# A gated linear recurrence and a spectral filter on one core: another DFT, other bonus path, other load path, other order

## The chip, the cores and the metric

The kernel runs on one core of a Trainium2 chip. A core has a matrix engine (PE, TensorE), a vector engine (DVE), a scalar engine (ACT), GpSimd (POOL), and SyncE (SP), whose queue issues the transfers here. Each engine runs its own queue in order; semaphores order the engines against one another. Matmul results land in PSUM; SBUF holds everything else. The metric is the time of one execution in microseconds.

## The reference, cut to what matters

```python
B, H, S, D = 4, 8, 768, 48
for t in range(S):                                   # per batch and head
    cur = einsum('bhd,bhe->bhde', u[None] * k[t], v[t])
    y[t] = einsum('bhd,bhde->bhe', r[t], state + cur)
    state = w[t][..., None] * state + einsum('bhd,bhe->bhde', k[t], v[t])
x = y as (B, S, 384)
x1, x2, x3 = split(x @ w_proj, 3)                    # three times 384 columns
conv = irfft(rfft(x2) * rfft(filter_fft))            # circular, over S = 768
out = (x1 * conv * x3) @ w_out
```

The term `u * k * v` of the present step is called the bonus: for a token and a head it is v times the number sum(r * u * k).

## The kernel before, in words

**Chunks.** The 768 tokens of a batch are six chunks of 128, so there are 24 chunks (0 to 23; chunk c belongs to batch c // 6). For each chunk SP loads w, k, r and v as [128 tokens, 8, 48] in fp32 (`ldw`, `ldk`, `ldr`, `ldv`, L384), into rings of five buffers. ACT takes the logarithm of w (`lw`); PE forms the running sums with triangular masks (`cs`, `ce`); ACT exponentiates (`en`, `eq`, `ph`, the last being the decay over the chunk); DVE or POOL multiply (`kh`, `q`); PE transposes both (`tqk`), a copy brings them to SBUF (`tT`), PE forms the scores (`sc`), DVE masks them (`mt`). The state goes from chunk to chunk by `kv` (PE) and `S` (DVE). The bonus is `rk` (r times k), `rku` (times u, L439), `cc` (a sum over 48 columns on DVE, L442), `vc` (times v, L448). `y` adds on PE the bonus (an identity matmul, L499), the state's part (L502) and the scores' part (L507). `xn` copies y, `yt` transposes it, `xT` stores it; for the second half of a batch `sa` and `sb` form the sum and the difference of the two halves of the sequence.

**The spectral part**, per batch, after its six chunks: `p1`, `p3` (products with w_proj, L539) and `x1`, `g` (their copies and their product); `x2` (L562) and `ab` for the sum and difference halves; `f` (L348, L356), the forward DFT as six row blocks ("slots") of 128 frequencies, real and imaginary ones in turn; `X` copies it. The filter's spectrum comes the same way, once: `ldfilt`, `fs`, `fd`, `hf`, `H`, `hg`. The product of two spectra is four products and two sums (`ua` to `ud`, L584; `pr`, L589; `pi`, L593), each 1152 columns wide for batches 0 to 2 and 384 for batch 3. The inverse DFT is `iE` and `iO` (L602), four matmuls each for each of three column blocks; `ec` copies, `s` and `d` (L617, L622) form the sum and difference, `yy` (L627) multiplies by the gate, `po` (L634) by w_out, `o` copies, `st` stores (L643). The basis of the inverse is made from that of the forward transform by transposes (`m2t`, L324).

**Order.** Nothing is ordered by loops: `ORDER` (L36) is a list of some 1070 words such as `P:po.1.3@3`, that is engine, operation, its indices, and for PE the PSUM bank. Each engine issues its words in the order in which they stand. Six banks are handed out by number, and two together hold the scores (`@8`). Waits follow from data, and from buffers that are used again. Eight matmuls on zeros run ahead of everything (L687). w_proj and w_out are loaded by POOL's queue, which converts them to bf16 on the way (L312, L317).

Of the kernel before, what the change touches and what calls it, by code (L numbers as in the profile page):

```python
# [20 lines left out]
L = 128  # L21
# [5 lines left out]
HALF = S // 2  # L27
NT = HALF // L
UNIT = 65536.0
NEG = -29952.0  # L30
WARM = 8

# [4 lines left out]
A:tLn0 S:ldu G:masks S:ldw1 S:ldk0 S:ldw0 G:iota S:ldw2 S:ldk2 V:ang2 S:ldk1 V:ang0 S:ldw3  # L37
V:ang1 S:ldv1 A:lw2 A:lw0 P:cs2@0 P:ce2@1 S:ldr1 P:ce0@2 A:eq2 A:lw1 S:ldr0 P:ce1@3 P:cs1@4
P:cs0@5 A:eq1 S:ldr2 A:eq0 A:en1 S:ldv0 A:en0 V:kh1 A:ph2 A:lw3 G:kh0 A:en2 S:ldk3 A:v1 V:kh2
A:ph0 A:sin S:ldw5 V:q0 V:rk0 P:tqk0@4 S:ldw6 V:q1 G:q2 V:tT0 S:ldv2 V:rku0 G:v0 P:tqk2@5 V:cc0  # L40
P:cs3@1 S:ldr3 V:rk2 P:kv0@0 G:vc0 P:sc0@8 V:S0 P:ce3@2 V:mt0 S:ldw4 G:rku2 A:tT2 G:rk1 S:ldv3
V:cc2 P:y0@4 A:lw5 P:sc2@8 A:eq3 V:xn0 P:tqk1@0 A:en3 S:ldk4 V:rku1 G:v2 A:ph1 P:yt0@5 P:cs5@4
V:cc1 P:kv1@1 A:xT0 V:mt2 S:ldk6 A:lw6 G:rk3 A:ph3 A:tT1 S:ldr4 V:S1 G:vc2 A:lw4 V:vc1 P:kv2@3
A:en5 G:q3 S:ldv4 P:sc1@8 V:kh3 P:cs6@5 P:cs4@2 P:ce6@0 A:en4 G:rku3 P:y2@1 S:ldw8 V:S2 P:ce5@4
V:xn2 A:eq5 S:ldr5 G:v3 A:eq6 V:mt1 P:yt2@2 G:kh4 P:ce4@3 A:ph6 P:tqk3@1 S:ldr6 A:eq4 V:cc3
G:rk4 A:xT2 P:y1@4 V:tT3 S:ldk5 A:xn1 V:q4 G:rku4 P:sc3@8 P:m2t3@0 S:ldw7 P:m2t0@2 V:mt3
P:tqk4@1 P:yt1@4 A:tT4 S:ldr8 V:m2c3a G:q5 V:cc4 A:en6 V:vc3 P:m2t5@1 S:ldv7 P:sc4@8 A:xT1 G:rk6
A:lw8 P:y3@5 A:ph4 A:m2c3b S:ldr7 V:kh5 P:ce8@4 A:xn3 P:cs8@3 V:v4 V:mt4 P:tqk5@0 G:vc4 S:ldv5
P:yt3@5 A:tT5 G:rk5 V:sa3 S:ldk8 V:sb3 A:lw7 P:kv3@0 A:eq8 S:ldv6 V:S3 G:kh6 A:xT3 A:m2c5
P:ce7@0 P:sc5@8 G:q6 S:ldw11 A:eq7 P:y4@5 V:mt5 P:kv4@1 G:rku5 A:xn4 S:ldw9 A:en8 P:m2t2@5  # L50
V:rku6 G:v5 A:m2c0 V:S4 P:yt4@3 S:ldk7 G:q7 P:tqk6@2 V:cc6 V:sa4 A:tT6 V:cc5 S:ldk9 G:kh8 V:sb4
V:vc5 A:v7 G:q8 S:ldv8 A:ph8 A:v6 V:xT4 A:lw11 V:rk8 P:kv6@1 A:m2c2a P:sc6@8 S:ldw10 G:ldwp
P:m2t4@2 P:cs7@4 P:y5@3 A:en7 S:ldr9 A:lw9 V:xn5 G:kh7 V:S6 P:yt5@4 P:cs9@3 G:rk7 P:tqk8@1 V:sa5
V:mt6 A:tT8 G:vc6 V:sb5 A:m2c2b G:v8 V:rku8 P:tqk7@1 A:xT5 G:rku7 P:ce9@5 A:en9 P:y6@4 A:m2c4
P:sc8@8 A:xn6 V:cc7 A:ph7 A:eq9 V:cc8 P:yt6@3 P:cs11@2 A:lw10 P:kv7@4 V:mt8 G:vc8 A:tT7 P:ce10@0
S:ldv9 V:vc7 A:xT6 P:sc7@8 V:S7 P:cs10@1 S:ldw12 P:ce11@3 V:kh9 A:en10 P:y8@4 V:mt7 A:ph9 A:en11
S:ldr10 A:eq11 P:p1.0.2.1@1 V:xn8 P:y7@5 V:x1.0.2.1 S:ldk10 G:rk9 P:p1.0.1.0@2 A:xn7 P:yt8@3
S:ldv10 A:xT8 P:yt7@4 V:v9 P:kv8@1 V:rku9 A:xT7 P:p1.0.0.1@5 V:S8 P:x2.0.1.1@3 S:ldr11 A:lw12
V:x1.0.1.0 P:kv9@4 A:x1.0.0.1 V:q9 P:x2.0.0.2@1 A:eq10 S:ldk11 V:ab.0.1.1 P:m2t1@2 P:x2.0.0.1@5
V:ab.0.0.2 P:p1.0.0.0@3 S:ldw14 G:rk10 P:p1.0.2.0@1 A:x1.0.0.0 V:x1.0.2.0 P:tqk9@3 S:ldv13 G:q10  # L60
# [48 lines left out]
V:sa21 P:p3.2.2.0@1 V:xT22 V:sb21 P:p1.3.2.0@2 V:ub.2.0 A:xT21 P:y23@0 V:g.2.2.0 P:po.0.2@4
V:X.2.4 A:x1.3.2.0 P:po.0.5@1 A:xn23 V:ua.2.0 G:uc.2.0 P:x2.3.1.1@5 P:iE.1.0@2 V:o.0.5 V:o.0.2  # L110
# [25 lines left out]
def kernel(  # L136
# [104 lines left out]
    def nth(c):  # L241
        return (c - c // NCH) % 3
# [477 lines left out]
```

## Time and profile before

| what | value |
|---|---|
| median of 3 runs | 187.91 us (187.36 to 188.9) |
| span of the profiled execution | 186.7 us; no other time is given for that execution |
| busy: PE, DVE, ACT, POOL | 154.7, 159.5, 117.3, 107.4 us |
| instructions | 4118 |
| moved by DMA | 26.41 MB |

A row of a group of instructions reads: line, engine, operation, output and inputs with their shapes, count, then busy time in us and the mean of one in ns, then the idle time of the engine just before them and what ended it. A window's row gives for a stretch of time the busy time of each engine with its number of instructions, then the granted clock of PE, the share of the time in which the 16 DMA engines were busy, and the traffic. A row of SP's queue gives start, duration, and the transfer issued.

### The profile page before, as it was taken

What the parts mean: (1) busy time and instruction counts of PE and PEld (TensorE: products, weight loads), DVE (VectorE), ACT (ScalarE), POOL (GpSimd) and SP (SyncE); (2) the same over time, 40 slices, a digit from 0 to 9 for tenths busy, and PEclk for the clock granted to TensorE, in tenths of its full rate; (3) what the DMA queues carried; (4) which work ended last, traced back from release to release, by engine and by line L of the source; (5) the groups of instructions that cost most, each with busy time, mean ns of one, the idle gap of its engine ahead of it and who ended that gap; (6) DMA issues with size and microseconds to landing.
All of it is one profiled execution on the core that took longest, in us unless ns stands there. A gap on an engine that the chain in (4) does not pass through costs nothing.

```text
span 186.7 us, 4118 instructions
## 1 busy us (share of the span) xinstructions
PE 154.7 (83%) x1526; PEld 97.8 (52%) x1526; DVE 159.5 (85%) x302; ACT 117.3 (63%) x257; POOL 107.4 (57%) x120
## 2 busy tenths in 40 slices
PE   5147787665799988897977799999999999999971
PEld 2115456444666546563655555756556655556630
DVE  6829989786989799989998979999998999699760
ACT  2289756976585497697486969988356415531532
POOL 6024899398651482995995636636651866781000
PEclk9999999995589999999999969999999999999999
DMA  4999999999999983999999890400001000335336
GB/s 104 202 219 201 192 188 205 199 177 197 193 195 188 213 172 76 196 191 214 176 248 241 172 203 5 63 4 0 0 4 42 0 0 4 126 125 214 130 144 235
DMA packets 105043, 26.41 MB, mean 141 GB/s; under 512 B 100288, under 2 KB 104640, under 8 KB 105024
## 3 DMA queue, kind: packets, MB, share of 16 engines
q1 hardware_dynamic: 104224, 24.98, 61.0%
q0 software_dynamic: 800, 1.18, 3.8%
q8 instruction: 12, 0.20, 0.4%
q14 instruction: 7, 0.06, 0.1%
HBM read 22.61 MB, written 4.72 MB: 146 GB/s over the span
## 4 chain that ended last, share of the span: by engine, by line
PE 56%; DVE 24%; ACT 9%; issue 4%; DMA 3%; SPq 2%; ACTq 0%
PE p L539 10%; PE po L634 6%; DVE mt L474 5%; PE iE L602 4%; PE iO L602 4%; PE f L356 4%; PE x L562 4%; ACT qkT L229 3%; PE tqk L454 3%; PE sc L467 3%; DVE cc L442 3%; PE y L507 2%; DVE S L492 2%; PE f L348 2%; DVE rku L439 2%
## 5 line engine op out<-in xcount | busy, mean ns | idle before, releaser
L539 PE MATMUL p<-xT,wproj 128*128 128x384 bf16 x144 | 30.0, 330 | 2.3 <-DVE S L492 2.0
L474 DVE TENSOR_TENSOR mt<-sc,mask_excl 128x1024 bf16<-128x1024 f32 x24 | 29.1, 1214 | 2.2 <-PE sc L467 2.2
L448 POOL TENSOR_TENSOR vc<-v,cc 128x384 bf16<-128x384 bf16 x19 | 16.8, 887 | 18.0 <-DVE cc L442 6.3
L430 POOL TENSOR_TENSOR qk<-ldk,en 128x384 bf16<-128x384 f32 x15 | 16.0, 1068 | 17.3 <-ACT phi L424 9.0
L436 POOL TENSOR_TENSOR rk<-ldr,ldk 128x384 bf16<-128x384 f32 x18 | 20.1, 1118 | 6.7 <-DVE rku L439 5.6
L229 ACT ACTIVATE qkT<-tqk 128x1024 bf16<-128x1024 bf16 x19 | 19.5, 1029 | 6.2 <-PE tqk L454 6.0
L454 PE MATMUL tqk<-ident,qk 128*128 128x128 bf16 x192 | 16.8, 238 | 5.0 <-POOL qk L430 2.1
L539 PEld LDWEIGHTS <-wproj 128*128 128x128 bf16 x144 | 13.0, 98 | 11.5 <-issue 4.4
L433 POOL TENSOR_TENSOR qk<-ldr,eq 128x384 bf16<-128x384 f32 x13 | 14.1, 1085 | 7.2 <-ACT eq L418 4.8
L229 ACT ACTIVATE x<-p 128x384 bf16<-128x384 f32 x20 | 9.6, 492 | 12.9 <-PE p L539 10.2
L454 PEld LDWEIGHTS <-qk 128*128 128x128 bf16 x192 | 13.2, 106 | 8.1 <-issue 4.0
L390 ACT ACTIVATE lg<-ldw 128x384 bf16<-128x384 f32 x24 | 12.7, 532 | 6.0 <-DMA ldw<-in_w_dram 5.9
L634 PE MATMUL po<-wout,y 128*128 128x384 bf16 x72 | 14.3, 326 | 1.3 <-DVE y L627 1.1
L412 ACT ACTIVATE en<-cs 128x384 f32<-128x384 f32 x24 | 11.7, 496 | 5.3 <-PE cs L394 5.2
L562 PE MATMUL x<-wproj,sd 128*128 128x384 bf16 x72 | 14.8, 326 | 0.0
L555 DVE TENSOR_TENSOR g<-p,x 128x384 bf16<-128x384 f32 x24 | 13.0, 549 | 1.8 <-PE p L539 1.8
L394 PE MATMUL cs<-lg,mask_incl 128*128 128x384 bf16 x24 | 9.5, 413 | 5.3 <-ACT lg L390 4.6
L418 ACT ACTIVATE eq<-ce 128x384 f32<-128x384 f32 x24 | 11.7, 495 | 3.1 <-PE ce L406 1.7
L492 DVE TENSOR_TENSOR S<-kv,phi 128x384 bf16<-128x384 f32 x20 | 11.0, 550 | 2.7 <-PE kv L485 2.2
L442 DVE TENSOR_REDUCE cc<-rku 128x8 f32<-128x384 bf16 x24 | 12.9, 541 | 0.1
L229 ACT ACTIVATE xn<-y 128x384 bf16<-128x384 f32 x17 | 8.4, 494 | 6.7 <-PE y L507 6.6
L602 PEld LDWEIGHTS <-P 128*128 128x128 bf16 x96 | 9.3, 98 | 6.1
(133 smaller groups left out, 410.2 us busy)
## 6 DMA issues: line engine op xcount, KB each, us to landing
ldw<-in_w_dram SPq DMA_DIRECT2D x24, 192.0 KB, 3.9
ldk<-in_k_dram SPq DMA_DIRECT2D x24, 192.0 KB, 3.8
ldv<-in_v_dram SPq DMA_DIRECT2D x24, 192.0 KB, 4.0
ldr<-in_r_dram SPq DMA_DIRECT2D x24, 192.0 KB, 3.9
out_dram<-o SPq DMA_DIRECT2D x12, 192.0 KB, 2.0
out_dram<-filt SPq DMA_DIRECT2D x12, 192.0 KB, 2.0
filt<-in_moe_filter_fft_dram SPq DMA_DIRECT2D x1, 1152.0 KB, 7.4
wproj<-in_moe_w_proj_dram POOLq DMA_DIRECT2D x1, 864.0 KB, 8.7
```

Source lines behind the costliest of these rows:

```text
L229: nc.scalar.activation(out=o, in_=i, func=AF.Copy)
L430: two(e).tensor_mul(qk_b[c % 3][:, 1, :, 0:D], ld["k"][c % 5], en_b[c % 3])
L436: two(e).tensor_mul(rk_b[c % 2], ld["r"][c % 5], ld["k"][c % 5])
L442: nc.vector.tensor_reduce(out=cc_b[c % 3], in_=rku_b[c % 2], axis=AX.X, op=ALU.add)
L448: two(e).tensor_mul(vc_b[c % 3], v_b[c % 4], cc_b[c % 3].to_broadcast([L, H, D]))
L454: nc.tensor.transpose(p[:, x, j, :], qk_b[c % 3][:, x, 2 * j:2 * j + 2, :], ident)
L474: nc.vector.tensor_mul(mt_b[c % 3], bank_of[f"sc{c}"].rearrange("p q j t -> p (q j) t"), dataclasses.replace(m[:, :], ap=[m[:, :].ap[0], [ ...
L492: nc.vector.tensor_mul(S_b[nth(c)], bank_of[f"kv{c}"], ph_b[nth(c)].to_broadcast([L, HP, 2, D]))
L539: nc.tensor.matmul(p, wproj[:, cb, col0:col0 + L], xT_b[b % 2][:, cb, sl], start=(cb == 0), stop=(cb == CB - 1),)
L562: nc.tensor.matmul(p, sd_b[q][0][:, cb, ti * L:(ti + 1) * L], wproj[:, cb, C:2 * C], start=(cb == 0), stop=(cb == CB - 1),)
L602: nc.tensor.matmul(p, P_b[q % 2][b % 2][:, q // 2, cb * L:(cb + 1) * L], m, start=(n == 0), stop=(n == len(slots) - 1),)
L634: nc.tensor.matmul(p, y_b[0][:, cb, ti * L:(ti + 1) * L], wout[:, cb, :], start=(cb == 0), stop=(cb == CB - 1),)
```

## The change

It does seven things at once:

1. **Half-sample DFT.** The time points of the transform are shifted by half a sample. Sum and difference of the halves go in as before, but the inverse uses the symmetry about the middle of each half: `i1` and `i2` take three slots each, so a batch has 18 matmuls in place of 24, and `d` writes its half in reverse. The filter's spectrum is turned by a phase to match (`ht`, `hr`, `hb`, `rot`).
2. **Spectrum products 768 wide.** With the filter's spectrum held twice (`TA`, `TB`), one frequency block takes `ua`, `ub` (X read twice) and `pp`, each 768 wide: nine passes a batch.
3. **Weights in fp32.** SP loads w_proj in three parts and w_out (`ldp`), and POOL or ACT convert them (`wc`). Angle tables share memory with the output buffers.
4. **Bonus of chunks 0 to 11 on PE.** `rk` is transposed (`rt`), copied (`rT`), multiplied by u laid out by head (`cu`), copied (`cv`). Chunks 12 to 23 keep `rku` and `cc`, but there the bonus is added to y by DVE (`xn`) and not by an identity matmul.
5. **Zeros.** 39 matmuls on zeros in ten places of the early order, in place of eight ahead of it.
6. `ph` is part of `eq`: ACT exponentiates eight more columns in the same instruction.
7. **A new order.** The filter and w_proj come in with the first chunks, and batch 0's spectral part runs beside the chunks of batches 1 and 2.

The core of the diff (the two lists of words are left out but for a few lines):

```diff
-    ld = {x: ring(f"ld{x}", 5, [L, H, D], FP32) for x in "wkrv"}
+    ld = {x: ring(f"ld{x}", LD, [L, H, D], FP32) for x in "wkrv"}
-    eq_b = ring("eq", 3, [L, H, D], FP32)
-    ph_b = ring("phi", 3, [L, HP, 2], FP32)
+    eq_b = ring("eq", 3, [L, C + 2 * HP], FP32)
...
+    fmap = filt.rearrange("p n c -> p (n c)")[:, 0:S]
+    ang = o0.rearrange("p n c -> p (n c)").bitcast(INT32)
+    fsd = UA.rearrange("p n a c -> p (n a c)").rearrange("p (a n c) -> p a n c", a=2, c=C)
...
-    def op_ldwp(e, k_):
-        nc.gpsimd.dma_start(out=wproj, in_=moe_w_proj.rearrange("(n p) f -> p n f", p=L))
+    def op_ldp(e, n):
+        src = moe_w_out if n == 3 else moe_w_proj[:, n * C:(n + 1) * C]
+        nc.sync.dma_start(
+            out=o0[:, 3 * (n % 2):3 * (n % 2) + 3, :], in_=src.rearrange("(n p) f -> p n f", p=L)
+        )
+    def op_wc(e, n):
+        copy(e, wout if n == 3 else wproj[:, n], o0[:, 3 * (n % 2):3 * (n % 2) + 3, :])
...
+    def op_rt(e, c, bank):
+        p = ps(f"rt{c}", bank, (L, CB, L), BF16)
+        f = rk_b[c % 2].rearrange("p h d -> p (h d)")
+        for cb in range(CB):
+            nc.tensor.transpose(p[:, cb, :], f[:, cb * L:(cb + 1) * L], ident)
+    def op_cu(e, c, bank):
+        p = ps(f"cu{c}", bank, (L, H))
+        for cb in range(CB):
+            nc.tensor.matmul(
+                p, rT_b[c % 2][:, cb, :], uh[:, cb, :], start=(cb == 0), stop=(cb == CB - 1)
+            )
...
     def op_xn(e, c):
-        copy(e, xn_b[c % 3], bank_of[f"y{c}"].rearrange("p h d -> p (h d)"))
+        nc.vector.tensor_add(
+            xn_b[c % 3], bank_of[f"y{c}"].rearrange("p h d -> p (h d)"),
+            vc_b[c % 3].rearrange("p h d -> p (h d)"),
+        )
...
+    def op_ua(e, b, n):
+        two(e).tensor_mul(UA[:, n], twice(X_b[0][:, n, :]), TA[:, n])
+    def op_ub(e, b, n):
+        two(e).tensor_mul(UB[:, n], twice(X_b[1][:, n, :]), TB[:, n])
+    def op_pp(e, b, n):
+        two(e).tensor_add(P_b[b % 2][:, n], UA[:, n], UB[:, n])
+    def inverse(name, bank, b, cb, slots):
+        p = ps(name, bank)
+        for i, s in enumerate(slots):
             nc.tensor.matmul(
+                p, P_b[b % 2][:, s // 2, s % 2, cb * L:(cb + 1) * L],
+                m_b[:, s].rearrange("p a t -> p (a t)"),
+                start=(i == 0), stop=(i == len(slots) - 1),
+            )
-    def op_iE(e, b, cb, bank):
-        inverse(f"iE.{b}.{cb}", bank, b, cb, (0, 1, 2, 3), 0)
-    def op_iO(e, b, cb, bank):
-        inverse(f"iO.{b}.{cb}", bank, b, cb, (2, 3, 4, 5), 1)
+    def op_i1(e, b, cb, bank):
+        inverse(f"i1.{b}.{cb}", bank, b, cb, (0, 2, 5))
+    def op_i2(e, b, cb, bank):
+        inverse(f"i2.{b}.{cb}", bank, b, cb, (1, 3, 4))
...
+    def op_z(e, n, bank):
+        p = ps(f"z{bank}", bank)
+        for _ in range(n):
+            nc.tensor.matmul(p, warm[:, 0:L], warm, start=True, stop=True)
...
+A:tLn S:ldu G:iota S:ldw0 P:z13@0 S:ldv1 G:masks S:ldw2 V:ang2 A:uc S:ldr0 G:iorot P:um@0 P:z5@1
...
+S:ldk20 V:cc16 A:v16 P:y15@2 A:o.0.5 V:mt17 P:ce18@0 S:ldr18 G:rku17 A:v18 P:ce20@1 P:cs20@3 A:eq20
+P:po.0.2@5 V:xn15 S:ldv19 A:en20 G:vc16 P:po.0.1@4 V:cc17 A:o.0.2 P:sc16@8 V:ua.1.2 A:lw21 S:st.0.2
```

More of the change, by code (lines that the diff above doesn't have):

```diff
@@ L27 @@
 HALF = S // 2
+QUART = S // 4
 NT = HALF // L
@@ L262, in op_iota @@
-        nc.gpsimd.memset(fmap[:, L:L + 1], float(HALF))
+        for rows, a0 in ((slice(0, DP), (0.0, 256.0, 1.0)), (slice(DP, L), (0.0, 129.0, 1.0))):
+            for j in (1, 2):
+                nc.gpsimd.tensor_scalar(
+                    out=fcol[rows, j:j + 1], in0=fcol[rows, j:j + 1], scalar1=a0[j], scalar2=None,
+                    op0=ALU.add,
+                )
+        straight, crossed = (0.75, 0.0, 0.5, 0.75), (0.0, 0.75, 0.25, 0.0)
+        for j in range(4):
+            nc.gpsimd.tensor_scalar(
+                out=rang[:, :, j], in0=fcol, scalar1=1.0 / (2 * S), scalar2=straight[j],
+                op0=ALU.mult, op1=ALU.add,
+            )
+            nc.gpsimd.tensor_scalar(
+                out=rang[DP:L, 1, j:j + 1], in0=fcol[DP:L, 1:2], scalar1=1.0 / (2 * S),
+                scalar2=crossed[j], op0=ALU.mult, op1=ALU.add,
+            )
@@ new lines, in op_wc, with op_mtr, mtr, op_mc @@
+    def op_wc(e, n):
+        copy(e, wout if n == 3 else wproj[:, n], o0[:, 3 * (n % 2):3 * (n % 2) + 3, :])
+    def op_mtr(e, a, bank):
+        p = ps(f"mtr{a}", bank, (L, 2, 2, L), BF16)
+        for q in (0, 1):
+            for ti in (0, 1):
+                nc.tensor.transpose(p[:, q, ti, :], slot_cols(ti, 2 * a + q), ident)
+    def mtr(a):
+        return bank_of[f"mtr{a}"].rearrange("p q a t -> p q (a t)")[:, :, 0:QUART]
+    def op_mc(e, a):
+        copy(e, m_b[:, 2 * a:2 * a + 2, 0, :], mtr(a))
@@ L333, in op_m2c, with op_ms @@
+    def op_ms(e, a):
+        o, i = m_b[:, 2 * a:2 * a + 2, 1, :], mtr(a)
+        sc = {0: 1.0, 1: sgn, 2: -1.0}[a]
+        if e == "A":
+            nc.scalar.activation(out=o, in_=i, func=AF.Copy, scale=sc)
         else:
-            copy(e, m2[:, n if n < 2 else n - 2, :], tp)
+            nc.vector.tensor_scalar(out=o, in0=i, scalar1=sc, scalar2=None, op0=ALU.mult)
     def op_fs(e, k_):
-        nc.vector.tensor_add(fs, filt[:, 0:NT, :], filt[:, NT:, :])
+        two(e).tensor_add(fsd[:, 0], filt[:, 0:NT, :], filt[:, NT:, :])
@@ L367, in op_H, with op_ht, op_hr @@
+    def op_ht(e, n, j):
+        src, dst, col = bank_of[f"hf{2 * n}"], E_b[j], rot[:, n, 2 * j:2 * j + 1]
         if e == "A":
-            nc.scalar.activation(out=dst, in_=bank_of[f"hf{q}"], func=AF.Copy, scale=sc)
+            nc.scalar.activation(out=dst, in_=src, func=AF.Copy, scale=col)
+        else:
+            nc.vector.tensor_scalar(out=dst, in0=src, scalar1=col, scalar2=None, op0=ALU.mult)
+    def op_hr(e, n, j):
+        nc.vector.scalar_tensor_tensor(
+            out=TA[:, n, j, :], in0=bank_of[f"hf{2 * n + 1}"],
+            scalar=rot[:, n, 2 * j + 1:2 * j + 2], in1=E_b[j], op0=ALU.mult, op1=ALU.add,
+        )
@@ L503, in op_y @@
                     p[:, 2 * j:2 * j + 2, :], qkT_b[c % 3][:, 0, j, :],
-                    S_b[nth(c - 1)][:, j], start=False, stop=False,
+                    S_b[nth(c - 1)][:, j], start=(j == 0 and not bonus), stop=False,
                 )
@@ L683 @@
         nc.vector.memset(scl0[0:1, :], 1.0 / S)
-        nc.vector.memset(m2x, 0.0)
-        hot = banks[0].tile([L, C], FP32, tag="a", name="hot")
-        for i in range(WARM):
-            nc.tensor.matmul(hot, warm[:, 0:L], warm, start=True, stop=True)
+        nc.vector.memset(sgn[0:DP, :], 1.0)
+        nc.vector.memset(sgn[DP:L, :], -1.0)
         for word in ORDER.split():
```

502 lines of the change are left out of this document (254 added, 248 removed).

## Prediction

> **What bounds the kernel now.** I read the page's head first, then the busy time of each engine in stretches, then the queue of the loads, and last the groups for prices.
>
> ```profile
> span 186.7 us, 4118 instructions
> ...
> PE 154.7 (83%) x1526; PEld 97.8 (52%) x1526; DVE 159.5 (85%) x302; ACT 117.3 (63%) x257; POOL 107.4 (57%) x120
> ...
> q0 software_dynamic: 800, 1.18, 3.8%
> ...
> PE 56%; DVE 24%; ACT 9%; issue 4%; DMA 3%; SPq 2%; ACTq 0%
> ```
>
> Two engines are busy for about 85% of the span and neither is idle for long, so the totals say little: the stretches decide. To cut the span I take the issue of the last load (SP's queue):
>
> ```profile
> 93.54 0.86 SPq L307 DMA_DIRECT2D filt<-in_moe_filter_fft_dram  x1
> ...
> 107.02 2.73 SPq L384 DMA_DIRECT2D ldv<-in_v_dram  x3
> ...
> 181.00 2.83 SPq L643 DMA_DIRECT2D out_dram<-filt  x6
> ```
>
> The last of three loads of v leaves at 109.7 us. Busy time on both sides of that point:
>
> ```profile
> core 0: us, PE busy (x) PEld busy (x) DVE busy (x) ACT busy (x) POOL busy (x), PEclk, DMA share, GB/s
> 0.00:8.40 8.40, 2.74 (x8) 1.14 (x9) 6.64 (x30) 1.76 (x3) 2.90 (x16) 1.00 0.72 147
> 8.40:50.00 41.60, 28.46 (x320) 19.59 (x320) 32.82 (x52) 29.91 (x63) 29.47 (x32) 0.92 1.01 197
> 50.00:109.70 59.70, 51.64 (x620) 33.91 (x619) 55.55 (x94) 44.06 (x104) 38.11 (x41) 0.96 0.94 191
> 109.70:176.00 66.30, 66.30 (x552) 40.35 (x551) 60.27 (x121) 37.34 (x83) 36.89 (x32) 0.99 0.20 57
> 0.00:109.70 109.70, 82.85 (x945) 54.64 (x946) 95.00 (x174) 75.73 (x167) 70.48 (x89) 0.94 0.95 190
> 109.70:186.70 77.00, 71.88 (x583) 43.20 (x581) 64.45 (x129) 41.60 (x91) 36.89 (x32) 0.99 0.23 72
> ```
>
> There are two stages. In the **head** (0 to 109.7) the DMA engines are busy for 0.95 of the time, 104.2 us, and DVE for 95.0; PE has only 82.9, so it loses 26.9 us there. In the **tail** (77.0 us) PE is bound: from 109.7 to 176.0 it has no idle time at all, and it loses 5.1 us in the whole tail. So PE waits for loads early and pays late. Work that moves from the tail into PE's 26.9 idle microseconds of the head is gained almost whole; work removed in the head is worth nothing unless the DMA engines or DVE shrink too.
>
> **The change part by part.** Prices of PE, from the chain of waits and the groups:
>
> ```profile
> 136.67 0.61 PE f L348 x6
> ...
> 171.15 0.49 PE po L634 x3
> ...
> 174.24 0.65 PE iO L602 x4
> L454 PE MATMUL tqk<-ident,qk 128*128 128x128 bf16 x192 | 16.8, 238 | 5.0 <-POOL qk L430 2.1 <-ACT qkT L229 1.2 <-ACT en L412 1.0
> L687 PE MATMUL hot<-warm 128*128 128x384 bf16 x8 | 2.7, 524 | 1.1 <-DVE warm L669 1.1
> L324 PE MATMUL m2t<-ident,F 128*128 128x128 bf16 x18 | 2.0, 233 | 1.3 <-ACT qkT L229 1.0 <-ACT xn L229 0.3
> ```
>
> A 384-column matmul in a stream costs 0.163 us (0.49 / 3), a group of three 0.49, the old inverse group of four 0.65, a small transpose 0.0875 (16.8 / 192).
>
> *Tail, PE.* I counted the words behind the last load of v in both written orders. Old: 24 inverse groups, 14 p1, 15 p3, 12 x2, 11 full and 5 split f, 24 po. New: 18 inverse groups, 6, 6, 7, 7 and 4, 18. That is 32 groups of three fewer (15.7), one split f (0.6), and the inverse goes from 24 x 0.65 = 15.6 to 18 x 0.49 = 8.8. The chunk work left (kv, sc, y) changes by about +0.4. PE in the tail: 71.9 - 15.7 - 0.6 - 6.8 + 0.4 = **49.2**.
>
> *Head, PE.* It takes the 32 groups that the tail loses and six inverse groups, 38 x 0.49 = 18.6; one split f, 0.6; the bonus of twelve chunks, 12 x 6 small transposes and matmuls at 0.0875 = 6.3. It loses the old warm-up (2.7), seven identity matmuls of y (1.1) and a little of the basis transposes (2.0, against 12 x 0.0875). Sum 82.9 + 18.6 + 0.6 + 6.3 - 2.7 - 1.1 - 0.9 - 0.5 = **103**. The zeros: 39 matmuls, 13 of them ahead of the first data; the other 26 cost 4.2 (0.163) to 8.8 us (2.74 / 8 = 0.34, the warm-up row). I cost them at nothing: they stand in the first 45 us, where PE idles now for 13 of 41.6 us. Without that cover they would add up to 8.8.
>
> DVE, ACT and POOL, prices from the groups:
>
> ```profile
> L442 DVE TENSOR_REDUCE cc<-rku 128x8 f32<-128x384 bf16 x24 | 12.9, 541 | 0.1
> L439 DVE TENSOR_TENSOR rku<-rk,u_bc 128x384 bf16<-128x384 bf16 x13 | 9.8, 751 | 0.1
> L555 DVE TENSOR_TENSOR g<-p,x 128x384 bf16<-128x384 f32 x24 | 13.0, 549 | 1.8 <-PE p L539 1.8
> L627 DVE TENSOR_TENSOR y<-SD,g 128x768 bf16<-128x768 bf16 x12 | 6.3, 550 | 0.0
> L617 DVE TENSOR_TENSOR SD<-iO,E 128x384 bf16<-128x384 f32 x12 | 6.3, 548 | 0.0
> L526 DVE TENSOR_TENSOR sd<-xT,yt 128x384 bf16<-128x384 bf16 x12 | 4.2, 346 | 1.0 <-PE yt L518 0.9
> L231 DVE COPY qkT<-tqk 128x1024 bf16<-128x1024 bf16 x5 | 3.4, 678 | 0.0
> L474 DVE TENSOR_TENSOR mt<-sc,mask_excl 128x1024 bf16<-128x1024 f32 x24 | 29.1, 1214 | 2.2 <-PE sc L467 2.2
> L229 ACT ACTIVATE ab<-x 128x384 bf16<-128x384 f32 x18 | 8.6, 491 | 4.5 <-PE x L562 4.3
> L424 ACT ACTIVATE phi<-ce 128x8 f32<-128x8 f32 x20 | 3.7, 183 | 1.9 <-DVE S L492 1.9
> L233 POOL CAST v<-ldv 128x384 bf16<-128x384 f32 x11 | 6.5, 591 | 0.0
> ```
>
> *Head, DVE.* Away: 13 reduces (7.0) and 12 rku (9.0; all twelve that remain go to POOL). New: 8 more g (4.4), 14 products of 768 columns at 0.55 (7.7), six sums and differences (3.3), three yy (1.7), seven passes that build the filter's spectrum (3.9), two hb (1.4, four copies at L526's price), two qkT and three rT copies (2.4). The rest about cancels (-2.8 in all). Net +6: 95.0 to **101**. ACT takes some 38 copies of 0.49 and loses 20 phi (3.7): 75.7 to about 93. POOL gains two 1152-wide casts (three times 0.59 each) and the constants: near 76. None of these is the longest.
>
> *Head, DMA.* Wproj and wout now travel as fp32 on SP's queue and not on POOL's, and filt leaves SP after 19 loads and not at 93.5; six stores of batch 0 come ahead of the last 11 loads.
>
> ```profile
> 93.50:102.50 9.00, 6.73 (x95) 4.70 (x93) 8.46 (x13) 6.60 (x16) 7.06 (x7) 1.00 0.98 249
> ```
>
> While filt moves, the traffic is 249 GB/s against 190 in the head, so rows of 1536 bytes cost less than the loads' 192. A weight block of 590 KB costs 2.4 us at 249 and 1.85 if all of that surplus is filt's; I take 2.0, four of them 8.0. The software queue's 3.8% of the span is 7.1 us, three quarters of it (wproj, 5.3) in the head. A store costs 0.47 (2.83 / 6) to 0.8 (197 KB at 249 GB/s), I take 0.7, six 4.2. DMA: 104.2 - 5.3 + 8.0 + 4.2 = **111**. Now the head is 5.5 us longer than its DMA work; with the same loss it is **117**. That is also PE's 103 plus 14 and DVE's 101 plus 16 (14.7 lost now).
>
> *Tail, DVE.* The old products there, from the windows of L584, L589 and L593, cost 13.6 us:
>
> ```profile
> 109.70:186.70 77.00, 10.96 (x17) 8.76 (x7) 0.99 0.23 72
> ...
> 109.70:186.70 77.00, 1.85 (x3) 4.20 (x3) 0.99 0.23 72
> ...
> 109.70:186.70 77.00, 0.75 (x1) 8.08 (x5) 0.99 0.23 72
> ```
>
> They become 16 of 0.55, 8.8. Also away: 8 g (4.4), six s and d (3.3), 14 copies X, ab, ec (7.7), six yy (3.3); new: five xn that add the bonus (2.8), one mt (1.2); the rest -2. DVE: 64.5 - 4.8 - 18.7 + 4.0 - 2 = **43**. PE's 49.2 plus 5.1 lost gives 54.3, DVE's 43 plus 12.5 gives 55.5. There is less independent work left to fill gaps, so I add 1.5: **57**.
>
> Sum: 117 + 57 = 174 of span. The median of the three runs, 187.91, is 1.2 over the profiled span of 186.7; so **175**.
>
> *Not shown by the trace.* The new products read X twice through a repeated outer dimension. Bounds: 0.55 (yy, the same width and types) and 0.95 (a DVE pass at one element per cycle, between g's 0.549 at 384 and mt's 1.214 at 1024 columns). I take yy's. The reversed write of d: it reads PSUM as now, so 0.55; a gain is excluded, and 1.1, twice the row, is the upper end (nine, 5 us). cv on 8 columns: 0.06 (the width's share of cc) to 0.183 (phi).
>
> The rule that bears on the products: the Trainium skill, page VectorE: DVE Perf Modes, section What auto-detection actually checks, says that the two-per-cycle mode is taken when all tensors are 16-bit with step one. By that the products keep 0.55; without it DVE grows by 20 x 0.4 = 8 us, and no row here shows it: the one repeated outer dimension in this trace, mt's mask, stands beside an fp32 operand.
>
> **The rivals.**
>
> 1. *Full overlap.* The weights run at filt's best rate and the DMA engines lose nothing: head 110, tail 54.5, time 166. For it: PE and DVE have 7 and 9 us to spare. Against: from 50 to 109.7 us the DMA engines lose 6% with less work on PE than the new head has.
>
> 2. *DVE is longer than thought.* The products fall to 0.95 (11 in the head, 9 in the tail, 8 us), or DVE is held up by POOL:
>
> ```profile
> 158.75 0.35 DVE L584 TENSOR_TENSOR Uc<-X,HI 128x384 bf16<-128x384 bf16 x1
> ...
> 159.48 0.88 DVE L584 TENSOR_TENSOR Ub<-X,HI 128x384 bf16<-128x384 bf16 x1
> 159.24 0.91 POOL L593 TENSOR_TENSOR P<-Uc,Ud 128x384 bf16<-128x384 bf16 x1 [1.34 <-DVE Uc L584]
> ```
>
> The same DVE form takes 0.35 alone and 0.88 beside a POOL product: it ends after POOL. Seven 768-wide POOL products (twice 0.91 each) stand in the new tail; if each holds a DVE product for half its length, that is 6 us. Against: the old tail had 15 POOL products. Either way 181 to 184. The Trainium skill, page SBUF — State Buffer, section Who interferes with whom, calls this an exclusive lock for two-input DVE work against POOL's reads; the trace agrees (0.88 against 0.35).
>
> 3. *Stores hold the loads.* SP's queue is in order and six stores of batch 0 now stand ahead of the last 11 loads.
>
> ```profile
> SPq L643 <- ACT X L229: 49.8, 2, 32.5
> ```
>
> Stores wait long now, but nothing is behind them. If the copies of po are 12 us late, the loads are too: 187, no change.
>
> 4. *Slower: the bonus's round trip.* For chunks 0 to 11 two POOL or DVE passes become transpose, copy, matmul, copy: four hops between three in-order queues, in a head where PE, DVE and DMA are within 10 us of each other. If each chunk holds its buffers, and with them the loads, 1.2 us longer, the head is 14 us longer and the time 190. It decides from 1.1 us a chunk. Against: the state's recurrence (kv, S) doesn't go through the bonus, only y does. That the change does nothing at all for the tail is excluded, as the moved groups can be counted.
>
> **How the numbers follow.** Forecast 175 (170 to 180): 0.52. Rival 1, 166: 0.15. Rival 2, 181 to 184: 0.15. Rival 3, 187: 0.07. Rival 4, 190: 0.11. Runs of one kernel spread by 0.8%, so 1% is about what can be told. Faster by over 1% (below 186.0): 0.52 + 0.15 + 0.15 = 0.82; within 1%: 0.07; slower: 0.11. The range 165 to 186 takes in the forecast, rivals 1 and 2 and both ends of the DMA and product prices; it leaves out rivals 3 and 4.
>
> **What would show it.** Right: the last load leaves near 117 us, PE has some 103 us behind it, the tail is near 57 with PE at 49. Products of 768 near 0.55. Wrong: DMA share well below 0.95 in the head (rival 3 or 4; then SP waits on ACT's o, or PE waits for rT and cv), a product near 0.95, or a tail in which PE idles for more than 8 us because batch 3's own chain is longer than its work.

## The result and the profile after

The changed kernel takes **164.96 us** (median of 4 runs, 164.77 to 165.35), the kernel before 187.89 beside it (187.36 to 188.9): ratio 0.877 (0.873 to 0.881), 22.9 us less. The profiled execution has a span of 163.2 us against 186.7. A few executions of these kernels fell in a slower state; the times and ratios below leave them out.

The page of the changed kernel, its head and the shares of the chain that ended last:

```profile
span 163.2 us, 4274 instructions
...
PE 147.6 (90%) x1590; PEld 93.6 (57%) x1590; DVE 149.5 (92%) x296; ACT 128.2 (79%) x266; POOL 108.0 (66%) x133
...
PE 40%; DVE 35%; issue 8%; ACT 6%; DMA 4%; SPq 3%; POOL 1%; DVEq 0%; POOLq 0%; ACTq 0%
```

The span fell by 23.5 us. DVE's work fell by 10 of it and its idle time by 13.5 (27.2 to 13.7); PE's busy time fell by 7 and its idle time by 16.4 (32.0 to 15.6). PE's busy time holds 10.7 us of zeros now (row below) and held 2.7 before, so its other work fell by 15.

SP's queue around the last loads, and the busy time on both sides of the point where the last load has been issued (114.4 us), in the columns of the windows shown before:

```profile
100.33 3.10 SPq L762 DMA_DIRECT2D out_dram<-o  x6
...
112.63 1.74 SPq L470 DMA_DIRECT2D ldv<-in_v_dram  x2
```

```profile
8.40:50.00 41.60, 35.97 (x426) 23.49 (x423) 36.75 (x67) 36.60 (x76) 21.71 (x27) 0.96 0.99 221
50.00:114.40 64.40, 61.80 (x748) 41.31 (x748) 63.78 (x113) 58.34 (x127) 54.13 (x55) 1.00 0.98 204
...
0.00:114.40 114.40, 104.78 (x1202) 67.90 (x1203) 106.98 (x214) 97.83 (x206) 82.38 (x111) 0.99 0.97 206
114.40:163.20 48.80, 42.80 (x392) 25.70 (x389) 42.50 (x83) 30.41 (x61) 25.57 (x22) 1.00 0.25 82
```

The head has become 4.7 us longer (109.7 to 114.4) and the tail 28.2 shorter (77.0 to 48.8). In the head PE has 104.8 us of work in place of 82.9. From 50 to 114.4 us DVE is busy for 63.8 of 64.4, PE for 61.8, and the DMA engines for 0.98: three resources are full at once, and the page alone doesn't say which of them sets the pace.

The products and the zeros, from the groups:

```profile
L769 PE MATMUL z<-warm 128*128 128x384 bf16 x39 | 10.7, 413 | 1.2 <-DVE warm L789 1.2
L699 DVE TENSOR_TENSOR UB<-X,TB 128x768 bf16<-128x768 bf16 x11 | 7.8, 712 | 0.0
L708 DVE TENSOR_TENSOR P<-UA,UB 128x768 bf16<-128x768 bf16 x10 | 5.8, 588 | 0.0
L696 DVE TENSOR_TENSOR UA<-X,TA 128x768 bf16<-128x768 bf16 x9 | 5.7, 644 | 0.0
```

### The profile page after: what moved, and what is told of

The parts are those of the page before. It is cut to its first block, busy times and chain, and to the rows that moved or that the text cites. A ratio compares the mean times of both kernels' runs of the same rounds, so it can differ in the third digit from the quotient of the medians.

```text
span 163.2 us, 4274 instructions
## 1 busy us (share of the span) xinstructions
PE 147.6 (90%) x1590; PEld 93.6 (57%) x1590; DVE 149.5 (92%) x296; ACT 128.2 (79%) x266; POOL 108.0 (66%) x133
## 4 chain that ended last, share of the span: by engine, by line
PE 40%; DVE 35%; issue 8%; ACT 6%; DMA 4%; SPq 3%; POOL 1%; DVEq 0%; POOLq 0%; ACTq 0%
PE p L655 7%; DVE mt L575 7%; PE i L714 5%; PE po L753 5%; PE f L426 4%; DVE qk L514 3%; PE tqk L555 3%; SPq L470 3%; DVE g L671 3%; PE f L419 2%; DMA ldk<-in_k_dram 2%; PE sc L568 2%; DVE S L594 2%; DMA out_dram<-o 2%; PE x L678 2%
## 5 line engine op out<-in xcount | busy, mean ns | idle before, releaser
L549 POOL TENSOR_TENSOR vc<-v,cc 128x384 bf16<-128x384 bf16 x21 | 19.2, 916 | 11.0 <-ACT v L236 4.5
L236 ACT ACTIVATE qkT<-tqk 128x1024 bf16<-128x1024 bf16 x17 | 17.4, 1026 | 0.8 <-PE tqk L555 0.6
L517 POOL TENSOR_TENSOR rk<-ldr,ldk 128x384 bf16<-128x384 f32 x15 | 16.5, 1102 | 0.0
L555 PE MATMUL tqk<-ident,qk 128*128 128x128 bf16 x192 | 15.2, 223 | 0.5 <-DVE qk L514 0.3
L714 PE MATMUL i<-m_b,P 128*128 128x384 bf16 x72 | 13.3, 326 | 0.0
L236 ACT ACTIVATE xT<-yt 128x384 bf16<-128x384 bf16 x22 | 10.5, 490 | 3.4 <-PE yt L634 2.1
L520 POOL TENSOR_TENSOR rku<-rk,u_bc 128x384 bf16<-128x384 bf16 x12 | 12.0, 1000 | 1.5 <-DVE cc L523 0.5
L236 ACT ACTIVATE X<-f 128x384 bf16<-128x384 f32 x22 | 10.7, 493 | 2.7 <-PE f L426 1.7
L236 ACT ACTIVATE x<-p 128x384 bf16<-128x384 f32 x22 | 10.7, 493 | 2.6 <-PE p L655 2.4
L505 ACT ACTIVATE eq<-ce 128x392 f32<-128x392 f32 (+1 forms) x24 | 11.9, 501 | 0.9 <-DVE qk L514 0.2
L769 PE MATMUL z<-warm 128*128 128x384 bf16 x39 | 10.7, 413 | 1.2 <-DVE warm L789 1.2
```

What stands on the lines that cost most here:

```text
L236: nc.scalar.activation(out=o, in_=i, func=AF.Copy)
L517: two(e).tensor_mul(rk_b[c % 2], ld["r"][c % LD], ld["k"][c % LD])
L549: two(e).tensor_mul(vc_b[c % 3], v_b[c % 4], cc_b[c % 3].to_broadcast([L, H, D]))
L555: nc.tensor.transpose(p[:, x, j, :], qk_b[c % 3][:, x, 2 * j:2 * j + 2, :], ident)
L714: nc.tensor.matmul(p, P_b[b % 2][:, s // 2, s % 2, cb * L:(cb + 1) * L], m_b[:, s].rearrange("p a t -> p (a t)"), start=(i == 0), stop=(i ...
```

## The experiments

First theory, the prediction's: the loads bound the head, and the change gains by moving PE's work from the tail beside them. Rival: DVE and PE, filled evenly by the new order, bound it. The parts of the change were also undone one by one. "After" is the changed kernel; each run is compared with the kernel before on the same chip.

**e1: the zeros.** Eight ahead of the data stay, the other nine places go.

```diff
-P:z13@0 ... P:z5@1 ... P:z4@3 ... P:z1@3
+P:z8@0
```

> The changed kernel with eight matmuls on zeros ahead of everything, as before, and none of the other 31. Theory (work of the matrix engine moved out of the tail, the head bound by the loads): the zeros stand where the matrix engine waits for loads, so 165 to 166.5 us. Rival (the clock): without them the matrix engine runs at half rate whenever it comes out of a wait, as the 0.53 us of a 384-column matmul before 53 us in the old kernel shows against 0.33 later; its first 35 us of work would take some 10 us longer: 170 to 175 us, and matmuls of 0.5 us in the first 50 us.

164.38 us, ratio 0.875 (0.867 to 0.884): taken together, the zeros neither gain nor cost anything. The rival's slow matmuls did come (384 columns took 0.48 to 0.53 us until 20 us, see the last section), and the time stayed where it was.

**e2: loads that are easy for the DMA engines.**

```diff
-            in_=src[b, :, ci * L:ci * L + L, :].rearrange("h t d -> t h d"),
+            in_=src[b].rearrange("h t d -> (h t d)")[ci * L * C:(ci + 1) * L * C].rearrange(
+                "(p h d) -> p h d", p=L, d=D),
```

> The loads of w, k, r and v fetch the same number of bytes as rows of 1536 bytes instead of rows of 192, so each chunk gets tokens and heads in another layout (the output is that of other inputs); everything else is unchanged. Theory (the head is bound by the loads, DMA share 0.97): a load costs 0.6 us instead of 0.95 and the last one leaves 5 to 25 us earlier than at 114.4 us; time 155 to 160 us. Rival (the head is bound by the vector engine, busy 9.8 of 10 us from 20 us on): DMA share falls to 0.7 or less, the time stays within 1.5 us of 165 us.

164.73 us, 0.876 (0.870 to 0.882). From 20 to 110 us, after and then e2:

```profile
20.00:110.00 90.00, 85.19 (x1043) 56.81 (x1040) 88.09 (x154) 80.11 (x174) 68.40 (x71) 1.00 0.97 210
```

```profile
20.00:110.00 90.00, 85.20 (x1048) 56.88 (x1049) 88.09 (x156) 79.81 (x176) 69.75 (x72) 1.00 0.59 196
```

```profile
107.40 0.91 SPq L470 DMA_DIRECT2D ldv<-in_v_dram  x2
```

The DMA engines' share falls from 0.97 to 0.59 and the last load leaves 6 us earlier, but DVE does the same 88.09 us of work in this stretch and the end stays, as the rival had it. **The loads alone don't set the pace**; the first theory falls. Long rows shorten the transfers and also their issue (0.91 us for the last two loads in place of 1.74), so "loads" means both here.

**e3: the bonus of chunks 0 to 11 by POOL and DVE again**, for each of these chunks c:

```diff
-P:rtc V:rTc P:cuc V:cvc
+V:rkuc V:ccc      (rku by POOL where rT was ACT's)
```

> Chunks 0 to 11 form the bonus as before (product with u on POOL, three of them on the vector engine, and a reduce on the vector engine) at the places of the two copies; transposes and small matmuls of the bonus are gone. Vector engine +7 us, POOL +9, matrix engine -7, scalar engine -5.6, all in the head. Theory (loads bound the head): 165 to 168 us. Rival (vector engine bounds the head): 171 to 173 us. If the matrix engine bounds the head: 160 to 163 us.

172.67 us, 0.921 (0.914 to 0.929): 7.7 us more. Groups of e3, and its busy time:

```profile
L518 POOL TENSOR_TENSOR rku<-rk,u_bc 128x384 bf16<-128x384 bf16 x21 | 20.8, 991 | 2.8 <-DVE rk L515 1.2 <-DVE cc L521 1.0
...
L521 DVE TENSOR_REDUCE cc<-rku 128x8 f32<-128x384 bf16 x24 | 12.9, 539 | 0.6 <-POOL rku L518 0.6
```

```profile
PE 150.1 (87%) x1518; PEld 93.1 (54%) x1518; DVE 156.7 (91%) x303; ACT 124.4 (72%) x250; POOL 118.2 (68%) x142
```

DVE has 7.2 us more, and the time grows by as much, as the rival had it (171 to 173). POOL has 10.2 us more as well and wasn't tried apart, but it is busy for only 68% and has 4% of the chain that ended last. The clock isn't the reason: of e3's runs the one with a mean granted clock of 0.989, near the changed kernel's 0.990, took 172.77 us.

**e4: the inverse with 24 matmuls** (in each group of three a fourth one on zeros):

```diff
-                start=(i == 0), stop=(i == len(slots) - 1),
+                start=(i == 0), stop=False,
             )
+        nc.tensor.matmul(
+            p, warm[:, 0:L], m_b[:, 0].rearrange("p a t -> p (a t)"), start=False, stop=True
+        )
```

> Each of the 24 groups of the inverse gets a fourth matmul, on zero weights, so that the matrix engine does as many as before (3.9 us more, 2.9 of it behind the last load). Theory (matrix engine bounds the tail): 168 us (plus 2.5 to 4). Rival (the vector engine or the latency of the last batch's own chain bounds the tail): 165 to 166 us.

168.19 us, 0.896 (0.888 to 0.905): 3.2 us more for 24 matmuls, at 0.163 us in a stream 3.9 of PE. The theory held: PE bounds the tail.

**e5: less work on DVE.** `mt` is 128x512 in place of 128x1024.

```diff
-            mt_b[c % 3], bank_of[f"sc{c}"].rearrange("p q j t -> p (q j) t"),
+            mt_b[c % 3][:, 0:HP, :], bank_of[f"sc{c}"][:, 0],
```

> The changed kernel with the mask laid over only four of the eight heads' scores (512 columns instead of 1024; the other four heads use the first four's): 24 times 0.55 us, 13 us, less on the vector engine, 10 of it ahead of the last load, all else the same. Theory now (the vector engine bounds the head, from 20 us on busy 9.8 of 10): 152 to 157 us. Rival (the matrix engine, busy 9.6 of 10, bounds as much): 161 to 165 us.

165.11 us, 0.883 (0.876 to 0.889): nothing, with 10.9 us less on DVE, so DVE alone doesn't set the pace either. Its last load and its busy time from 20 to 110 us:

```profile
113.27 1.87 SPq L470 DMA_DIRECT2D ldv<-in_v_dram  x2
```

```profile
20.00:110.00 90.00, 85.15 (x1042) 57.16 (x1043) 78.81 (x156) 78.47 (x174) 69.31 (x71) 0.98 0.97 211
```

DVE has 9.3 us less in this stretch, and the last load leaves no earlier, at 115.1 us, with the DMA engines at 0.97.

**e6: less work on PE.** `proj` runs over two of the three blocks of its contraction.

```diff
-        for cb in range(CB):
+        for cb in range(CB - 1):
```

> The changed kernel with two of the three contraction blocks in p1 and p3: 48 matmuls, 7.8 us, less on the matrix engine, 5.9 us of it ahead of the last load and 2.0 behind. Theory (vector engine bounds the head; the tail is bound by both): 163 to 165 us. Rival (matrix engine bounds): 157 to 160 us.

164.39 us, 0.878 (0.871 to 0.886): nothing, with 5.3 us less on PE. That lies in the theory's range, but e5 took away its reason, DVE alone.

**e7: the order without the cheaper work.** New order, half-sample transform and 768-wide products stay; the bonus is made as before in all chunks, the inverse has a fourth matmul on zeros, only eight of the zeros ahead of the data stay, the weights travel on POOL's queue.

```diff
-P:rtc V:rTc P:cuc V:cvc ... P:ybc ... V:xnc
+G:rkuc V:ccc ... P:yc ... A:xcc
-        nc.sync.dma_start(out=o0[:, ...], in_=src.rearrange("(n p) f -> p n f", p=L))
+        nc.gpsimd.dma_start(out=wout if n == 3 else wproj[:, n], in_=src.rearrange(...))
```

> The new order and the half-sample transform with the other parts undone: bonus of all chunks by product and reduce and an identity matmul in y, y copied (nine of the last twelve on the scalar engine), four matmuls in each inverse group, eight zeros in front, weights converted on POOL's queue. If the parts add up (the bonus alone 7.7 us, the inverse alone 3.2, the identity matmuls about 1.5): 176 to 179 us, so that the order holds some 10 of the 22.7 us. Rival (the order is worth little by itself, the engines' smaller work is the gain): 184 to 188 us. Rival (the order is nearly all): 168 to 171 us.

180.21 us, 0.962 (0.954 to 0.970), outside all three ranges and nearest to the first: with what stays in, the new order gives 7.8 us of the 23 (7.2 by the ratio). The other 15.2 come from the smaller work on top of it. If the parts add up, which no run shows, e3 and e4 account for 7.7 and 3.2, and 4.3 remain for the identity matmuls of y and the weights' queue, which were not taken apart.

**e8 and e9: the same cuts on the kernel before**, the long rows of e2 and the half mask of e5.

> The kernel before with its loads of w, k, r and v as rows of 1536 bytes (same bytes, other tokens). The prediction took the old head (DMA share 0.95) as bound by the loads: then the last load leaves 8 to 30 us earlier and the time is 170 to 181 us. Rival (the vector engine bounds the old head, the loads only follow): 186 to 188 us.

> The kernel before with the mask applied to four of the eight heads: DVE falls from 159 to about 148 us. If DVE's stream bounds the head of the kernel before (95 of 110 us busy there, loads not the bound as e8 showed), the head gets 4 to 9 us shorter: 179 to 184. Rival, the chain of each chunk (hops between engines) in the written order bounds it: the cut gives under 2 us, 186 to 188.

e8: 187.0 us, 0.995 (0.990 to 1.000), though its last load leaves 5.3 us earlier (104.4 us in place of 109.7). e9: 184.22, 0.981 (0.975 to 0.987), 3.4 us less, just above the range for a bound by DVE. So the loads alone didn't bind the old head either; DVE did in part, and much of it was neither.

**e11: less on DVE and PE together** (e5 and e6 in one kernel).

> The changed kernel with the mask applied to four of the eight heads (as in e5) and with p1 and p3 contracting two of three blocks (as in e6): DVE 11 us and PE 5 us less together. Theory, DVE and PE bind in turn: taken together the cuts save what neither saved alone, 158 to 162 us. Rival, the end is set by the chain of each chunk and by ACT (128 us busy, 9 of 10 in the middle): 164 to 166, as with either cut alone.

165.35 us, 0.882 (0.877 to 0.887): again nothing, against the theory that these two bind in turn. But e11's own page and waits show what came instead, the shares of the chain and two rows of its waits (engine, line, who it waited for; us, times, longest):

```profile
PE 24%; DMA 20%; DVE 17%; POOL 13%; ACT 11%; issue 7%; SPq 6%; POOLq 0%; DVEq 0%; ACTq 0%
```

```profile
ACT v L236 <- DMA ldv<-in_v_dram: 5.5, 3, 2.2
POOL v L240 <- DMA ldv<-in_v_dram: 4.2, 4, 2.2
```

and the same wait in the changed kernel:

```profile
ACT v L236 <- DMA ldv<-in_v_dram: 0.2, 1, 0.2
```

With DVE and PE lighter, the engines wait for loads. Hence a new theory: loads, DVE and PE tie in the head.

**e12: zeros in the kernel before**, one matmul ahead of each PE word up to the first projection, 60 in all.

```diff
-P:cs2@0 P:ce2@1 ...
+P:z1@0 P:cs2@0 P:z1@1 P:ce2@1 ...
```

> The kernel before with one matmul of zeros ahead of each PE word until the first projection (60 matmuls in the first 55 us, in PE's idle time). Theory: in the kernel before PE's idle time makes matmuls of 384 columns take 0.53 us there instead of 0.33, and other engines have time to spare early, so the zeros repair the duration (maximum of cs and p from 0.53 to 0.34) and save nothing or up to 2 us: 186 to 188.5. Rival, half-rate matmuls are the reason for the head of the kernel before: 181 to 184. Other rival: the zeros are in the way of PE's chains: 190 or more.

200.5 and 200.6 us, 1.070 (1.063 to 1.076): the theory missed and the second rival held. The group of the zeros in e12:

```profile
L649 PE MATMUL z<-warm 128*128 128x384 bf16 x60 | 22.6, 377 | 3.1 <-ACT qkT L230 2.4 <-DVE S L493 0.6
```

Of 22.6 us of zeros 13 reached the end, though PE idled for 19 us of the first 55 in the kernel before:

```profile
0.00:55.00 55.00, 35.96 (x385) 24.02 (x386) 43.33 (x87) 35.84 (x73) 35.14 (x51) 0.91 0.97 190
```

The zeros repaired only part of the slow matmuls: those from 43 to 53 us are fast now (a `cs` of 0.32 in place of 0.53), those of the first 28 us are not (`cs` up to 0.50). The likely reason for the loss, not tried by itself, is that there most of PE's words follow one another in chains with the other engines, so that an idle share is no room for work at a given place. Whether the zeros waited for the PSUM banks that they write wasn't tried apart.

**e13 to e16: all three made lighter, and each left in place.** e13 is e11 with long rows; e14 keeps all of PE's work, e15 all of DVE's; e16 is e9 with long rows.

> e11 (mask over half of the heads, p1 and p3 with two of three blocks) with loads of 1536-byte rows as in e2, which take other elements of the inputs. Theory, loads, DVE and PE tie in the head: with all three smaller it falls for the first time, by 5 to 10 us: 155 to 160. Rival, the hops of each chunk and the written order set the head: 163 to 166, as in e2, e5, e6 and e11.

> The changed kernel with half of the mask (DVE 11 us less) and loads of 1536-byte rows, which take other elements; PE has all its work. If three resources tie, PE still holds: 161 to 165. If PE is no bound, the time falls as far as in e13: 155 to 160.

> The changed kernel with p1 and p3 of two blocks (PE 5 us less) and loads of 1536-byte rows, which take other elements; DVE has all its work. If three resources tie, DVE still holds: 163 to 165. If DVE is no bound, the time falls as far as in e13: 155 to 160.

> The kernel before with half of the mask (as in e9, which gave 3.6 us) and loads of 1536-byte rows (as in e8, which gave 0.9). If loads and DVE hold its head in turn, both together give more than the sum of 4.5: 178 to 182. If the chain of hops holds it, they give the sum or less: 183 to 186.

| kernel | lighter | us | ratio (interval) |
|---|---|---|---|
| after | nothing | 164.96 | 0.877 (0.873 to 0.881) |
| e2 | loads | 164.73 | 0.876 (0.870 to 0.882) |
| e5 | DVE | 165.11 | 0.883 (0.876 to 0.889) |
| e6 | PE | 164.39 | 0.878 (0.871 to 0.886) |
| e11 | DVE, PE | 165.35 | 0.882 (0.877 to 0.887) |
| e15 | PE, loads | 163.73 | 0.873 (0.867 to 0.879) |
| e14 | DVE, loads | 160.31 | 0.854 (0.849 to 0.860) |
| e13 | DVE, PE, loads | 158.13 | 0.843 (0.837 to 0.848) |
| e9 | before: DVE | 184.22 | 0.981 (0.975 to 0.987) |
| e16 | before: DVE, loads | 184.05 | 0.982 (0.973 to 0.991) |

From 20 to 110 us e14, then e13, and the chains of e14 and e15:

```profile
20.00:110.00 90.00, 87.13 (x1080) 59.18 (x1078) 82.57 (x163) 82.67 (x182) 72.51 (x73) 1.00 0.62 201
```

```profile
20.00:110.00 90.00, 85.00 (x1066) 56.47 (x1065) 84.76 (x167) 82.97 (x186) 73.73 (x75) 1.00 0.60 200
```

```profile
PE 62%; DVE 18%; issue 7%; ACT 5%; POOL 5%; POOLq 0%; DVEq 0%; ACTq 0%
```

```profile
DVE 45%; PE 20%; ACT 13%; DMA 12%; issue 7%; SPq 1%; DVEq 0%; ACTq 0%
```

**Loads and DVE are tied**: either alone gives nothing, both give 4.7 us (4.3 by the ratios). PE is the next limit: e14's chain is 62% PE, and with PE lighter too (e13) another 2.2 go. With DVE's work in place (e15) the chain is DVE's and the fall, 1.2 us, lies within the intervals. The rival of hops and written order would have held e13 at 163 or more, and e13 is at 158. e14 fell between its two ranges, lower than a tie of three would have it (161 to 165): PE stands a few us behind the other two, not level with them. In the kernel before long rows add nothing to the half mask (e16 against e9), as the rival had it: there was no such tie.

No version that beats the changed kernel followed: it would have to lighten the loads and DVE together with the computation kept, and none of these runs does that.

## Why the prediction was off

Its forecast of 174 us of span came out at 163.2: 2.6 in the head (117 against 114.4), **8.2 in the tail** (57 against 48.8).

*The step that failed: "Tail, PE", the term 49.2.* It measured 42.8, and these 6.4 are most of the 8.2; for the time that PE loses in the tail the 57 left 7.8 us, and the run lost 6.0. The term took PE's busy time behind the last load from the trace (71.9) and subtracted words counted behind that load in the written orders. But SP runs ahead of PE in the list, and by how much differs. PE of the kernel before and then after, at the load's issue (109.7 and 114.4):

```profile
109.30 1.17 PE L356 MATMUL f<-ab,F 128*128 128x384 bf16 x3
...
117.52 0.33 PE L518 MATMUL yt<-ident,xn 128*128 128x128 bf16 x3
```

```profile
115.22 0.65 PE L426 MATMUL f<-ab,F 128*128 128x384 bf16 x3
115.80 0.40 PE L568 MATMUL sc<-qkT 48*128 48x128 bf16 x8
```

The first word listed behind the load is `yt18` before and `sc19` after. Before, PE reached it 7.8 us after the load's issue, so 7.8 of the 71.9 were words listed ahead of it; after, 1.4. The difference, 6.4, is the whole error of the term. Behind that word PE was busy for 64.1 us before and 41.4 after:

```profile
117.52:186.70 69.18, 64.06 (x506) 38.60 (x501) 58.27 (x117) 35.40 (x77) 31.68 (x26) 1.00 0.22 74
```

```profile
115.80:163.20 47.40, 41.40 (x375) 24.81 (x374) 41.10 (x80) 29.01 (x59) 25.13 (x22) 1.00 0.23 79
```

That is 22.7 less, just what the term subtracted (15.7 + 0.6 + 6.8 - 0.4). About half of the 7.8 us, 3.6 of busy time, is the forward transform of the filter (`hf`): it runs from 111.6 to 115.7 us before and from 32.7 to 40 us after, so it left the tail, and the count of words, in which it stands ahead of the load both times, didn't see it. The forecast and rival 1's time both have this term in them. A count by list place can be subtracted from a count by list place only.

*Head.* The sum of the DMA work came out: 0.97 of 114.4 is 111, the predicted 111; its terms weren't measured one by one. That the loads set the head, this work plus a loss of 5.5, is the second step that failed: the lost time fell to 3.4, and e2 shows that DMA work can go without the end moving, because DVE holds it (in the kernel before, e8 shows it too). That 117 lay within 2.6 of the measured 114.4 is partly luck, as DVE's work filled the head too (63.8 of its last 64.4 us). "Work removed in the head is worth nothing unless the DMA engines or DVE shrink too" was too weak: **both** must shrink.

The engines' work in the head was sized less well. PE was predicted at 103 (the last 0.5 of its sum has no source there) and measured 104.8, but 10.7 of that are zeros, costed at nothing; its other work is 94.1. Part of the 8.9 less is that the groups of the chunks cost less there (160 small transposes of `tqk` 14.3 us before, 163 of them 13.0 after; 22 `cs` 8.6, 24 of them 7.7); the rest wasn't traced. ACT measured 97.8 against 93, and the prediction's own terms (75.7 + 18.6 - 3.7) give 90.6. POOL measured 82.4 against 76, DVE 107.0 against 101. Of DVE's 6.0 the products are only 0.5: in the head twelve of them cost 8.2 us, where 14 had been priced at 7.7. More is work of the chunks: eight `q` took 7.3 us in place of 5.6, and eight `rk` 6.6, where five took 4.5.

*The products.* Their medians are at yy's price, their means are not (UB of the changed kernel, minimum, median and maximum in ns):

```profile
L699 DVE TENSOR_TENSOR UB<-X,TB x11: 536/543/1614, 53.9 to 145.8; 128x768 bf16<-128x768 bf16 x11
```

So the repeated outer dimension doesn't cost the fast mode. The Trainium skill, VectorE: DVE Perf Modes, section What auto-detection actually checks, by which 16-bit tensors of step one keep two elements a cycle, agrees with 543 ns. The means are longer where POOL works beside them: the longest, 1.614 us at 137.7, ends just after a 768-wide product of POOL. So rival 2's second half was real, at 3.0 us over all 30 products (19.3 of busy time against 30 times 0.543), half of the 6 that the rival took for it.

*Tail, DVE*: 43 predicted, 42.5 measured.

*Rivals.* Rival 1's time (166) was nearly right by luck: its head was 4.4 too short (110 against 114.4) and its tail 5.7 too long (54.5 against 48.8), so that two errors cancelled, and its reason (weights at the best rate, no DMA loss) isn't borne out. Rival 3: six stores of batch 0 are issued in 3.10 us at 100.3, with no wait for `o` in SP's queue. Rival 4: the bonus on PE is no round trip that holds anything; undoing it costs 7.7 us (e3). The text saw in it nothing but a saving of 16 us on DVE that new work takes up again; with DVE tied, it is the largest of the three parts that were undone singly (zeros, bonus, inverse).

*Zeros at nothing*: right in the time (e1). Idle time in the first 45 us is only part of the reason: with 8.0 us of zeros gone PE's busy time fell by 5.1 only (147.6 to 142.5), as its other matmuls took longer, and neither reached the end. Idle time doesn't hide zeros anywhere (e12).

*The offset* between span and median was 1.8 us, not 1.2.

## What to carry to other kernels

Where an order has been balanced, cutting one resource tells nothing: cut one, then two, then three, and read from the chain's shares which comes up next; here loads and DVE tie and only both together gave time. Undoing a part works the other way and can show, since work added to a tied resource lengthens the whole (in e3, 7.2 us more of DVE, with 10.2 more of POOL, cost 7.7). When work is moved across a cut, price both sides in executed work at the same instant, or both in list order, never one from each.

## What the hardware showed

The same bytes in rows of 1536 rather than 192 bytes took 0.59 of the DMA engines' time in place of 0.97 (e2, 20 to 110 us), all other traffic included. The Trainium skill, DMA: Bandwidth & Descriptors, section Why small descriptors are slow (HBM only), gives a fixed cost per packet as the reason; the direction agrees, the cause was not tried.

Matmuls of 384 columns can take 1.6 times as long early on. `cs` in the kernel before, in e1 (eight zeros) and after:

```profile
L394 PE MATMUL cs<-lg,mask_incl x24: 322/336/527, 8.5 to 116.8; 128*128 128x384 bf16 x24
```

```profile
L479 PE MATMUL cs<-lg,mask_incl x24: 323/326/481, 5.8 to 112.8; 128*128 128x384 bf16 x24
```

```profile
L480 PE MATMUL cs<-lg,mask_incl x24: 322/326/337, 7.5 to 113.6; 128*128 128x384 bf16 x24
```

The longest `cs` is 0.53 us before, 0.48 in e1 and 0.34 after. The clock column needs care here. In e1 it reads 1.00 from the start, and yet the matmuls of 384 columns are slow until 20 us:

```profile
0.00:20.00 20.00, 12.52 (x101) 8.24 (x102) 14.99 (x54) 14.62 (x25) 11.52 (x38) 1.00 0.88 178
```

```profile
17.88 0.49 PE L485 MATMUL ce<-lg,mask_excl 128*128 128x384 bf16 x1
...
22.28 0.33 PE L485 MATMUL ce<-lg,mask_excl 128*128 128x384 bf16 x1
```

The trace of e1 has no record of the clock before 20.4 us of the span, and the column counts time without a record as full clock. The first record is at 29.3 us in the kernel before and at 7.2 us after. Where there are records, they and the durations agree: in the kernel before the clock is halved from 42.9 to 53.2 us, and `cs` takes 0.53 us at 46.95 (the row of 35 to 50 us shows a clock of 0.76).

```profile
35.00:50.00 15.00, 9.25 (x110) 6.93 (x109) 11.54 (x20) 9.89 (x21) 13.24 (x15) 0.76 0.99 190
```

```profile
46.95 0.53 PE L394 MATMUL cs<-lg,mask_incl 128*128 128x384 bf16 x1
...
54.29 0.34 PE L394 MATMUL cs<-lg,mask_incl 128*128 128x384 bf16 x1
```

The Trainium skill, TensorE: Matmul & The Clock Gate, Part 1, says that an idle array falls to half rate and a busy stretch of some 3.4 us lifts it. The durations and the records agree with that, and e1's time (164.38 against 164.96) shows that for this kernel it makes no difference.
